# Second matmul layer as seven Strassen products in 32-column tiles of the array

## Chip, cores, metric

One core of one Trainium2 chip. The metric is device time in microseconds (us) of one execution. Ratios between kernels are computed as the mean time of one kernel's fast runs over the mean of the other's of the same rounds, so they are not quite the ratio of the medians quoted here.

## The reference, cut to what matters

```python
# attention part: a causal 7-tap convolution over time, weights by head; gives x (32768 x 192)
def _moe_ref(x, w_in, w_out):          # w_in 192 x 2048, w_out 2048 x 192
    h = x @ w_in
    relu6 = np.clip(h + 3.0, 0.0, 6.0)
    g = h * relu6 / 6.0
    return (g @ w_out).astype(np.float32)
```

Everything is computed in fp32. `w_in` and `w_out` arrive as fp64 and are converted on the chip, in the start.

## The kernel before

The tokens go through in 32 blocks of 1024, each as two halves of 512 (k = 0, 1). A block has two stages. The first layer makes h for 16 chunks of 128 hidden channels; two 64-row tiles of the array run beside each other (431 ns for two records of 593 ns each), one for each half. ScalarE and VectorE turn h into g. The second layer takes 128 tokens of g as the stationary operand (the one that is loaded first, 128 x 128, in 191 ns) and streams 192 columns of `w_out` past it. In this stage VectorE computes the seven taps of the next block's convolution. Matmuls write their sums into PSUM; a bank of it is, in this document, the 512 fp32 columns of one of the program's buffers. ScalarE or VectorE reads them out.

```python
def bank():
    return ps.tile([P, N], F32, name="bank")        # ps: 8 buffers of one PSUM bank each

def h_unit(i, c):                                    # first layer, one chunk
    hs = [bank() for _ in range(G)]
    for s in range(K3):
        for k in range(G):
            r = slice(k * D2, (k + 1) * D2)
            nc.tensor.matmul(out=hs[k][:], lhsT=w_in[r, slots[k], s, :], rhs=y[r, s, :],
                             start=(s == 0), stop=(s == K3 - 1))                        # L223
    for k in range(G):
        r6 = rs.tile([P, N], F32, name="r6")
        nc.scalar.activation(r6[:], hs[k][:], ACT.Relu, bias=half[:], scale=1.0 / 6.0)  # L229
        nc.vector.scalar_tensor_tensor(out=g_tiles[i][k][:, c, :], in0=r6[:], scalar=1.0,
                                       in1=hs[k][:], op0=ALU.min, op1=ALU.mult)         # L232

def unit(t):                                         # second layer, 128 tokens
    o = bank()
    for c in range(NC):
        nc.tensor.matmul(out=o[:, 0:D], lhsT=g[k][:, c, tk * P : (tk + 1) * P],
                         rhs=w_out[:, c, :], start=(c == 0), stop=(c == NC - 1))        # L250
    nc.scalar.copy(out=st["sb"][:, t % TO, :], in_=o[:, 0:D])
    # ... one store of 384 KB after every fourth unit
```

## Time and profile before

| | before |
|---|---|
| median of the first three runs | 2757.02 us (2756.26 to 2757.45) |
| TensorE busy | 2685.9 of 2756.4 us |
| one block in mid-run | 41.40 us first layer + 41.80 us second layer |
| VectorE busy in a block | 33.2 us |
| the rest of the span (start, first block's delay, tail) | 94 us |

TensorE never waits after the start (its 66.6 us of idle time all lie in the first 140 us), so only less TensorE work, or faster streaming, can make the kernel faster. The prediction below shows the lines. In a line of groups one reads: source line, engine, operation, output<-input, shapes, count | busy us, mean ns of one | idle time before and what ended it. PE is TensorE, PEld its weight loads, DVE VectorE, ACT ScalarE, POOL GpSimd.

### The profile page before, as it was taken

The numbers are of one execution on the slowest core, as the hardware profiler recorded it, in microseconds if no ns is written. First come the engines' busy times: TensorE is split into PE (matmuls) and PEld (weight loads), VectorE is DVE, ScalarE is ACT, GpSimd is POOL, SyncE is SP. The second block draws the span as 40 slices with busy tenths as digits, with TensorE's granted clock in tenths as the row PEclk, the third lists the DMA queues.
The fourth block names the chain that finished last, engine by engine and source line by source line (L and its number), as shares of the span: only waits on it lengthen the run. The fifth ranks groups of instructions, "written<-read, shape, count | busy, mean of one in ns | idle before, by whom it ended". The sixth has DMA issues, their size and how long they took to land.

```text
span 2756.4 us, 32856 instructions
## 1 busy us (share of the span) xinstructions
PE 2685.9 (97%) x14336; PEld 1934.2 (70%) x14336; DVE 1096.8 (40%) x1327; ACT 741.2 (27%) x1298; POOL 65.4 (2%) x52
## 2 busy tenths in 40 slices
PE   5599999999999999999999999999999999999999
PEld 2377776677766677766677766677766777766777
DVE  5533344333344233444233444333443333443331
ACT  2222233322233322233322233222233222233222
POOL 3500000000000000000000000000000000000000
PEclk9699999999999999999999999999999999999999
DMA  3200000000000000000000000000000000000000
GB/s 81 69 24 24 17 13 18 24 24 24 11 19 18 24 24 24 7 24 18 24 24 24 7 24 18 23 24 24 7 18 24 24 24 24 7 18 24 12 12 12
DMA packets 54176, 60.57 MB, mean 22 GB/s; under 512 B 2832, under 2 KB 41744, under 8 KB 54032
## 3 DMA queue, kind: packets, MB, share of 16 engines
q1 hardware_dynamic: 48384, 52.17, 6.8%
q10 hardware_dynamic: 5648, 6.30, 0.8%
q8 instruction: 112, 1.84, 0.3%
q14 instruction: 32, 0.26, 0.0%
HBM read 31.72 MB, written 25.17 MB: 21 GB/s over the span
## 4 chain that ended last, share of the span: by engine, by line
PE 96%; POOL 2%; DVE 1%; DMA 1%; issue 0%; ACT 0%; ACTq 0%; POOLq 0%; DVEq 0%
PE bank L250 48%; PE bank L223 48%; POOL scale L132 1%; POOL scale L136 1%; DVE y L199 0%; DMA w_in<-w_in 0%; POOL w_out L151 0%; DVE scale L147 0%; DMA stage<-in_moe_w_in_dram 0%; POOL w_in L151 0%; ACT r L229 0%; DVE g L232 0%; ACTq L76 0%; DVE y L195 0%; DVE scale L128 0%
## 5 line engine op out<-in xcount | busy, mean ns | idle before, releaser
L250 PE MATMUL bank<-w_out,g 128*128 128x192 f32 x8192 | 1349.3, 328 | 29.3 <-POOL w_out L151 29.3
L223 PE MATMUL bank<-y,w_in 64*128 64x512 f32 x6144 | 1340.9, 593 | 37.3 <-DVE y L199 26.1
L250 PEld LDWEIGHTS bank<-w_out,g 128*128 128x128 f32 x8192 | 1336.3, 191 | 57.2 <-POOL w_out L151 33.7
L232 DVE SCALAR_TENSOR_TENSOR g<-r,bank 128x512 f32<-128x512 f32 x1024 | 658.0, 683 | 1563.9 <-ACT r L229 1563.7
L223 PEld LDWEIGHTS bank<-y,w_in 64*128 64x128 f32 x6144 | 597.9, 188 | 760.8 <-issue 743.8
L229 ACT ACTIVATE r<-bank,half 128x512 f32<-128x512 f32 x1024 | 649.7, 684 | 739.7 <-PE bank L223 734.7
L254 ACT COPY o_sb<-bank 128x192 f32<-128x192 f32 x256 | 81.7, 319 | 1237.1 <-PE bank L250 1237.1
L199 DVE SCALAR_TENSOR_TENSOR y<-x,c_sb,y 128x1536 f32<-128x1536 f32 x192 | 349.2, 1819 | 6.8
L195 DVE TENSOR_SCALAR y<-x,c_sb 128x1536 f32<-128x1536 f32 x32 | 57.7, 1802 | 0.0
L132 POOL TENSOR_SCALAR scale<-scale 128x384 uint32<-128x384 uint32 x16 | 25.1, 1569 | 55.6 <-DVE scale L128 55.6
L136 POOL TENSOR_SCALAR scale<-scale 128x384 uint32<-128x384 uint32 x16 | 24.1, 1503 | 1.3
L147 DVE SCALAR_TENSOR_TENSOR scale<-stage,scale 128x384 uint32<-128x384 uint32 x16 | 8.9, 558 | 35.1 <-POOL scale L136 35.1
L127 ACT ACTIVATE rest<-stage 128x384 f32<-128x384 uint32 x16 | 8.7, 549 | 28.5 <-DVE scale L128 17.3
L140 DVE TENSOR_SCALAR top<-stage 128x384 uint32<-128x384 uint32 x16 | 11.3, 703 | 0.0
L144 DVE SCALAR_TENSOR_TENSOR sig<-top,rest 128x384 f32<-128x384 uint32 x16 | 10.6, 660 | 1.6
L151 POOL TENSOR_TENSOR w_out<-sig,scale 128x384 f32<-128x384 f32 x8 | 8.3, 1035 | 5.4 <-DVE scale L147 5.4
L151 POOL TENSOR_TENSOR w_in<-sig,scale 128x384 f32<-128x384 f32 x8 | 8.0, 996 | 5.4 <-DVE scale L147 5.4
L128 DVE TENSOR_SCALAR scale<-stage 128x384 uint32<-128x384 uint32 x16 | 5.6, 353 | 1.2 <-DMA stage<-in_moe_w_in_dram 1.2
L173 ACT ACT_TABLE_LOAD x1 | 1.3, 1283 | 5.5 <-issue 5.5
L168 DVE TENSOR_REDUCE mx<-w_sb 128x1 f32<-128x7 f32 x1 | 0.2, 159 | 6.5 <-DMA w_sb<-in_weight_dram 6.5
L68 DVE MEMSET x<- 64x18 f32 x8 | 0.6, 73 | 0.8 <-PEq L304 0.8
L173 ACT ACTIVATE e_sb<-e_sb 128x7 f32<-128x7 f32 x1 | 0.2, 208 | 1.0 <-DVE e_sb L170 1.0
(10 smaller groups left out, 1.3 us busy)
## 6 DMA issues: line engine op xcount, KB each, us to landing
out_dram<-o_sb SPq DMA_DIRECT2D x64, 384.0 KB, 2.5
x<-in_x_dram SPq DMA_DIRECT2D x56, 388.5 KB, 5.8
x<-in_x_dram SPq DMA_DIRECT2D x8, 384.0 KB, 4.7
stage<-in_moe_w_in_dram ACTq DMA_DIRECT2D x16, 192.0 KB, 3.6
stage<-in_moe_w_out_dram ACTq DMA_DIRECT2D x8, 384.0 KB, 3.1
w_in<-w_in SPq DMA_DIRECT2D x16, 96.0 KB, 2.2
w_sb<-in_weight_dram ACTq DMA_DIRECT2D x2, 1.8 KB
```

Of the source, the lines that this page charges most:

```text
L132: nc.gpsimd.tensor_scalar(out=scale[:], in0=scale[:], scalar1=float((1023 - 127) << 20), scalar2=0.0, op0=ALU.subtract, op1=ALU.max,)
L136: nc.gpsimd.tensor_scalar(out=scale[:], in0=scale[:], scalar1=float(255 << 20), scalar2=8.0, op0=ALU.min, op1=ALU.mult,)
L140: nc.vector.tensor_scalar(out=top[:], in0=high, scalar1=0xFFFFF, scalar2=0x100000, op0=ALU.bitwise_and, op1=ALU.bitwise_or,)
L144: nc.vector.scalar_tensor_tensor(out=sig[:], in0=top[:], scalar=2.0**-20, in1=rest[:], op0=ALU.mult, op1=ALU.add)
L151: nc.gpsimd.tensor_tensor(out=dst, in0=sig[:], in1=scale[:].bitcast(F32), op=ALU.mult)
L195: nc.vector.tensor_scalar(out=y[:], in0=x[:, :, 0:N], scalar1=c, scalar2=None, op0=ALU.mult)
L199: nc.vector.scalar_tensor_tensor(out=y[:], in0=x[:, :, k : k + N], scalar=c, in1=y[:], op0=ALU.mult, op1=ALU.add,)
L223: nc.tensor.matmul(out=hs[k][:], lhsT=w_in[r, slots[k], s, :], rhs=y[r, s, :], start=(s == 0), stop=(s == K3 - 1),)
L229: nc.scalar.activation(r6[:], hs[k][:], ACT.Relu, bias=half[:], scale=1.0 / 6.0)
L232: nc.vector.scalar_tensor_tensor(out=g_tiles[i][k][:, c, :], in0=r6[:], scalar=1.0, in1=hs[k][:], op0=ALU.min, op1=ALU.mult,)
L250: nc.tensor.matmul(out=o[:, 0:D], lhsT=g[k][:, c, tk * P : (tk + 1) * P], rhs=w_out[:, c, :], start=(c == 0), stop=(c == NC - 1),)
L254: nc.scalar.copy(out=st["sb"][:, t % TO, :], in_=o[:, 0:D])
```

## The change

The product g @ w_out is cut two by two: A11, A12 are the two hidden halves of g for the tokens of half 0, A21, A22 those for half 1; B11 to B22 are quarters of `w_out`, C11 to C22 quarters of the result. One level of Strassen's algorithm (in Winograd's form) then needs seven products instead of eight, so 7/8 of the streaming. It pays with four operand sums S1 to S4 on VectorE, four differences T1 to T4 of `w_out` on GpSimd (once), and the sums of the products. Now g moves and `w_out` stands, in pieces of 32 columns, four of them side by side in the array. The result comes out transposed and is turned in 32 x 32 blocks on VectorE. The products come in six groups of matmuls, 0 to 5, each filling one PSUM bank, b[0] to b[5].

```diff
-    ps = ctx.enter_context(tc.tile_pool(name="ps", bufs=8, space=bass.MemoryType.PSUM))
+    ps = ctx.enter_context(tc.tile_pool(name="ps", bufs=4, space=bass.MemoryType.PSUM))
...
+        for o, x, y in ((T1, B12, B11), (T3, B22, B12), (T2, B22, T1), (T4, T2, B21)):
+            nc.gpsimd.tensor_tensor(out=w[:, o], in0=w[:, x], in1=w[:, y], op=ALU.subtract)
...
-    def bank():
-        return ps.tile([P, N], F32, name="bank")
+    def banks():
+        return ps.tile([P, 2, N], F32, name="banks")
...
+    def s_unit(p):                       # after every fourth first-layer unit
+        r = slice(p, p + 2)
+        for o, x, y, op in (
+            (S1, A21, A22, ALU.add), (S3, A11, A21, ALU.subtract),
+            (S2, S1, A11, ALU.subtract), (S4, A12, S2, ALU.subtract),
+        ):
+            nc.vector.tensor_tensor(out=o[:, r], in0=x[:, r], in1=y[:, r], op=op)
+
+    prod = {
+        1: (A11, B11), 2: (A12, B21), 3: (S4, B22), 4: (A22, T4),
+        5: (S1, T1), 6: (S2, T2), 7: (S3, T3),
+    }
...
+                out=bank[j * QS : (j + 1) * QS], lhsT=w_out[:, p, w, cols], rhs=x[:, p],
+                start=(p == ks[0]), stop=(p == ks[-1]), tile_position=(0, j * QS),
...
+        ba, bb, bc = banks(), banks(), banks()
+        b = [t[:, k] for t in (ba, bb, bc) for k in range(2)]
+        def three(k, n, n4, q4):         # three pieces of product n, one of product n4
+            side_by_side(*[out_mm(b[k], q, n, q, every) for q in range(NQ)],
+                         out_mm(b[k], NQ, n4, q4, every))
...
+        three(0, 1, 2, 0)
+        nc.scalar.copy(out=p1[:], in_=b[0][m])
+        piece(p2, 0, b[0], NQ)           # ScalarE copy of 32 rows
+        three(1, 5, 2, 1)
+        piece(p2, 1, b[1], NQ)
+        for u in conv:
+            u()
+        three(2, 7, 2, 2)
+        piece(p2, 2, b[2], NQ)
+        ...                              # sum, transpose and store of C11
+        three(3, 6, 4, 0)
+        ...                              # copy, four sums that read b[3], b[2], b[1]; store of C22
+        three(4, 3, 4, 1)
+        piece(p4, 1, b[4], NQ)
+        add(u2[:], u2[:], b[4][m])
+        ...                              # store of C12; last piece of product 4 into b[5], C21
```

The first layer's unit writes both halves into one two-bank buffer, with one ReLU and one product 1024 wide; g, x and y are kept in one buffer each.

More of the change, by code (lines that the diff above doesn't have):

```diff
@@ L50 @@
     assert H * GJ == D2 and K3 * GJ == GS and G == 2 and S % TB == 0 and DFF % P == 0 and PAD <= N
-    cst = ctx.enter_context(tc.tile_pool(name="cst", bufs=1))
-    xs = ctx.enter_context(tc.tile_pool(name="xs", bufs=2))
-    ys = ctx.enter_context(tc.tile_pool(name="ys", bufs=2))
-    gs = ctx.enter_context(tc.tile_pool(name="gs", bufs=G + 1))
-    rs = ctx.enter_context(tc.tile_pool(name="rs", bufs=3))
-    os_ = ctx.enter_context(tc.tile_pool(name="os", bufs=2))
-    stg = ctx.enter_context(tc.tile_pool(name="stg", bufs=3))
-    cnv = ctx.enter_context(tc.tile_pool(name="cnv", bufs=2))
-    ps = ctx.enter_context(tc.tile_pool(name="ps", bufs=8, space=bass.MemoryType.PSUM))
+    NP = NC // 2
+    DH = D // 2
+    QS = 32
+    NQ = DH // QS
+    assert NQ * QS == DH and NQ == 3 and P // QS == 4
+    cst = ctx.enter_context(tc.tile_pool(name="cst", bufs=1))
+    xs = ctx.enter_context(tc.tile_pool(name="xs", bufs=1))
+    ys = ctx.enter_context(tc.tile_pool(name="ys", bufs=1))
+    rs = ctx.enter_context(tc.tile_pool(name="rs", bufs=2))
+    ps = ctx.enter_context(tc.tile_pool(name="ps", bufs=4, space=bass.MemoryType.PSUM))
+    start_pools = ExitStack()
+    stg = start_pools.enter_context(tc.tile_pool(name="stg", bufs=3))
+    cnv = start_pools.enter_context(tc.tile_pool(name="cnv", bufs=2))
     def load_x(i):
@@ L86 @@
     w_in = cst.tile([P, NC, K3, P], F32, name="w_in")
-    w_out = cst.tile([P, NC, D], F32, name="w_out")
+    w_out = cst.tile([P, NP, 8, DH], F32, name="w_out")
+    B11, B12, B21, B22, T1, T2, T3, T4 = range(8)
     w_in_bits = moe_w_in.bitcast(U32).rearrange("(p s) (c f w) -> c p s f w", s=K3, f=P, w=2)
-    w_out_bits = moe_w_out.bitcast(U32).rearrange("(c p) w -> p c w", p=P)
-    WO = 2
+    w_out_bits = moe_w_out.bitcast(U32).rearrange("(k c p) w -> p c k w", p=P, k=2)
     WS = K3 * P
-    assert WO * D == WS
+    assert 2 * D == WS
     def stage():
@@ L102, in load_w_in @@
                 out=st[half * D2 : (half + 1) * D2].rearrange("p (s f) w -> p s (f w)", s=K3),
-                in_=w_in_bits[2 * j + half].rearrange("p s f w -> p s (f w)"),
+                in_=w_in_bits[j + half * NP].rearrange("p s f w -> p s (f w)"),
             )
@@ L109, in load_w_out @@
         nc.scalar.dma_start(
-            out=st[:].rearrange("p (c d) w -> p c (d w)", c=WO),
-            in_=w_out_bits[:, j * WO : (j + 1) * WO],
+            out=st[:].rearrange("p (k d) w -> p k (d w)", k=2), in_=w_out_bits[:, j]
         )
@@ L153, in w_in_unit @@
     def w_in_unit(j):
-        own, other = j, NC // 2 + j
+        own, other = j, NP + j
         to_f32(w_in[:, own].rearrange("p s f -> p (s f)"), w_in_st.pop(j))
@@ L159, in w_out_unit @@
     def w_out_unit(j):
-        dst = w_out[:, j * WO : (j + 1) * WO, :].rearrange("p c d -> p (c d)")
-        to_f32(dst, w_out_st.pop(j))
+        w = w_out[:, j]
+        to_f32(w[:, B11 : B22 + 1].rearrange("p b d -> p (b d)"), w_out_st.pop(j))
+        for o, x, y in ((T1, B12, B11), (T3, B22, B12), (T2, B22, T1), (T4, T2, B21)):
+            nc.gpsimd.tensor_tensor(out=w[:, o], in0=w[:, x], in1=w[:, y], op=ALU.subtract)
     w_in_st, w_out_st = {}, {}
@@ L204, in conv_units @@
         return [lambda k=k: tap(k) for k in range(KC)]
-    g_tiles = {}
-    def bank():
-        return ps.tile([P, N], F32, name="bank")
+    g = cst.tile([P, NP, 2, G, N], F32, name="g")
+    A11, A21, A12, A22 = (g[:, :, h, k] for h in range(2) for k in range(G))
+    s_t = cst.tile([P, 3, NP, N], F32, name="s")
+    S1, S2, S4 = (s_t[:, j] for j in range(3))
+    S3 = A21
+    def banks():
+        return ps.tile([P, 2, N], F32, name="banks")
     def h_unit(i, c):
         y = y_tiles[i]
-        slots = [c // 2 + (c % 2 != k) * (NC // 2) for k in range(G)]
-        hs = [bank() for _ in range(G)]
+        slots = [c % NP + (c // NP != k) * NP for k in range(G)]
+        h = banks()
         for s in range(K3):
@@ L223, in h_unit @@
                 nc.tensor.matmul(
-                    out=hs[k][:], lhsT=w_in[r, slots[k], s, :], rhs=y[r, s, :],
+                    out=h[:, k], lhsT=w_in[r, slots[k], s, :], rhs=y[r, s, :],
                     start=(s == 0), stop=(s == K3 - 1),
                 )
-        for k in range(G):
-            r6 = rs.tile([P, N], F32, name="r6")
-            nc.scalar.activation(
-                r6[:], hs[k][:], ACT.Relu, bias=half[:], scale=1.0 / 6.0
-            )
-            nc.vector.scalar_tensor_tensor(
-                out=g_tiles[i][k][:, c, :], in0=r6[:], scalar=1.0, in1=hs[k][:],
-                op0=ALU.min, op1=ALU.mult,
-            )
@@ L237, in out_units @@
-    def out_units(i):
-        g = g_tiles.pop(i)
-        rows = out[i * TB : (i + 1) * TB, :].rearrange("(t p) d -> p t d", p=P)
-        TO = NT // 2
-        st = {}
-        def unit(t):
-            if t % TO == 0:
-                st["sb"] = os_.tile([P, TO, D], F32, name="o_sb")
-            o = bank()
-            k, tk = divmod(t, N // P)
-            for c in range(NC):
-                nc.tensor.matmul(
-                    out=o[:, 0:D], lhsT=g[k][:, c, tk * P : (tk + 1) * P],
-                    rhs=w_out[:, c, :], start=(c == 0), stop=(c == NC - 1),
-                )
-            nc.scalar.copy(out=st["sb"][:, t % TO, :], in_=o[:, 0:D])
-            if t % TO == TO - 1:
-                nc.sync.dma_start(out=rows[:, t + 1 - TO : t + 1, :], in_=st["sb"][:])
-        return [lambda t=t: unit(t) for t in range(NT)]
+        r6 = rs.tile([P, G, N], F32, name="r6")
@@ new lines, in h_unit @@
+        nc.scalar.activation(r6[:], h[:], ACT.Relu, bias=half[:], scale=1.0 / 6.0)
+        nc.vector.scalar_tensor_tensor(
+            out=g[:, c % NP, c // NP], in0=r6[:], scalar=1.0, in1=h[:],
+            op0=ALU.min, op1=ALU.mult,
+        )
+    def s_unit(p):
[5 more added lines that the diff above has]
+            nc.vector.tensor_tensor(out=o[:, r], in0=x[:, r], in1=y[:, r], op=op)
@@ new lines, with out_mm @@
+    prod = {
+        1: (A11, B11), 2: (A12, B21), 3: (S4, B22), 4: (A22, T4),
+        5: (S1, T1), 6: (S2, T2), 7: (S3, T3),
+    }
+    def out_mm(bank, j, n, q, ks):
+        x, w = prod[n]
+        cols = slice(q * QS, (q + 1) * QS)
+        return [
+            lambda p=p: nc.tensor.matmul(
+                out=bank[j * QS : (j + 1) * QS], lhsT=w_out[:, p, w, cols], rhs=x[:, p],
+                start=(p == ks[0]), stop=(p == ks[-1]), tile_position=(0, j * QS),
+            )
+            for p in ks
+        ]
@@ new lines, in side_by_side, with out_phase, piece, add @@
+    def side_by_side(*streams):
+        for mms in zip(*streams):
+            for mm in mms:
+                mm()
+    def out_phase(i, conv):
+        every = range(NP)
+        ba, bb, bc = banks(), banks(), banks()
+        b = [t[:, k] for t in (ba, bb, bc) for k in range(2)]
+        def three(k, n, n4, q4):
+            side_by_side(
+                *[out_mm(b[k], q, n, q, every) for q in range(NQ)],
+                out_mm(b[k], NQ, n4, q4, every),
+            )
+        def piece(dst, q, src, j):
+            nc.scalar.copy(
+                out=dst[q * QS : (q + 1) * QS], in_=src[j * QS : (j + 1) * QS]
+            )
+        def add(out, x, y, op=ALU.add):
+            nc.vector.tensor_tensor(out=out, in0=x, in1=y, op=op)
+        def store(c, k, half_):
+            xt = ot.tile([DH, N], F32, name="xt")
+            nc.vector.transpose(out=xt[:], in_=c)
+            t0 = i * TB + k * N
+            rows = out[t0 : t0 + N, half_ * DH : (half_ + 1) * DH].rearrange(
+                "(t r) (q d) -> q r t d", r=QS, d=QS
+            )
+            for q in range(NQ):
+                nc.sync.dma_start(
+                    out=rows[q],
+                    in_=xt[q * QS : (q + 1) * QS].rearrange("r (t d) -> r t d", d=QS),
+                )
+        m = slice(0, DH)
+        p1, p2, p4, u2, u3, c22 = (cs.tile([DH, N], F32, name=f"c{k}") for k in range(6))
+        three(0, 1, 2, 0)
[7 more added lines that the diff above has]
+        piece(p2, 2, b[2], NQ)
+        add(p2[:], p1[:], p2[:])
+        store(p2[:], 0, 0)
+        three(3, 6, 4, 0)
+        piece(p4, 0, b[3], NQ)
+        add(u2[:], p1[:], b[3][m])
+        add(u3[:], u2[:], b[2][m])
+        add(u2[:], u2[:], b[1][m])
+        add(c22[:], u3[:], b[1][m])
+        store(c22[:], 1, 1)
+        three(4, 3, 4, 1)
+        piece(p4, 1, b[4], NQ)
+        add(u2[:], u2[:], b[4][m])
+        store(u2[:], 0, 1)
+        n = NP // 4
+        side_by_side(*[out_mm(b[5], j, 4, 2, range(j * n, (j + 1) * n)) for j in range(4)])
+        piece(p4, 2, b[5], 0)
+        last = p4[2 * QS : 3 * QS]
+        for j in range(1, 4):
+            add(last, last, b[5][j * QS : (j + 1) * QS])
+        add(u3[:], u3[:], p4[:], ALU.subtract)
+        store(u3[:], 1, 0)
@@ L265 @@
         for i in range(NB):
-            g_tiles[i] = [gs.tile([P, NC, N], F32, name="g") for _ in range(G)]
-            conv = conv_units(i + 1) if i + 1 < NB else []
-            for c in range(NC):
-                if i == 0 and c % 2 == 0:
-                    j = c // 2
-                    if j + 2 < NC // 2:
-                        w_in_st[j + 2] = load_w_in(j + 2)
-                    else:
-                        w_out_st[j + 2 - NC // 2] = load_w_out(j + 2 - NC // 2)
-                    if j + 1 < NC // 2:
-                        w_in_unit(j + 1)
-                h_unit(i, c)
-            y_tiles.pop(i)
+            for p in range(NP):
+                if i == 0:
+                    if p + 2 < NP:
+                        w_in_st[p + 2] = load_w_in(p + 2)
+                    else:
+                        w_out_st[p + 2 - NP] = load_w_out(p + 2 - NP)
+                    if p + 1 < NP:
+                        w_in_unit(p + 1)
+                h_unit(i, p)
+                h_unit(i, NP + p)
+                if p % 2:
+                    s_unit(p - 1)
+            y_tiles.pop(i)
+            if i == 0:
+                for j in range(NP):
+                    if j + 2 < NP:
+                        w_out_st[j + 2] = load_w_out(j + 2)
+                    w_out_unit(j)
+                start_pools.close()
+                cs = ctx.enter_context(tc.tile_pool(name="cs", bufs=1))
+                ot = ctx.enter_context(tc.tile_pool(name="ot", bufs=4))
+            out_phase(i, conv_units(i + 1) if i + 1 < NB else [])
             if i + 2 < NB:
                 x_tiles[i + 2] = load_x(i + 2)
-            if i == 0:
-                for j in range(NC // WO):
-                    if j + 2 < NC // WO:
-                        w_out_st[j + 2] = load_w_out(j + 2)
-                    w_out_unit(j)
-            for t, u in enumerate(out_units(i)):
-                u()
-                for v in conv[t * len(conv) // NT : (t + 1) * len(conv) // NT]:
-                    v()
 _INS = ['x', 'weight', 'moe_w_in', 'moe_w_out']
```

## The prediction

> **What bounds the kernel now.** I read the page's busy times first, then the groups, then the busy times by window for one whole block (1024 tokens), then the waits.
>
> ```profile
> PE 2685.9 (97%) x14336; PEld 1934.2 (70%) x14336; DVE 1096.8 (40%) x1327; ACT 741.2 (27%) x1298; POOL 65.4 (2%) x52
> L250 PE MATMUL bank<-w_out,g 128*128 128x192 f32 x8192 | 1349.3, 328 | 29.3 <-POOL w_out L151 29.3
> L223 PE MATMUL bank<-y,w_in 64*128 64x512 f32 x6144 | 1340.9, 593 | 37.3 <-DVE y L199 26.1
> ```
>
> TensorE is busy for 97% of the span, split evenly between the first layer (L223) and the second (L250), and its only idle time, 29.3 + 37.3 us, is in the start. The windows of one block in mid-run (first layer, then second) give the period:
>
> ```profile
> 256.50:297.90 41.40, 41.40 (x194) 18.51 (x193) 19.27 (x30) 19.30 (x31) 0.00 (x0) 1.00 0.11 29
> 297.90:339.70 41.80, 41.80 (x260) 41.58 (x258) 13.93 (x10) 3.50 (x9) 0.00 (x0) 1.00 0.03 10
> ```
>
> The columns are length, then the busy time of PE, weight loads, VectorE, ScalarE and GpSimd, the clock, DMA. A block is 41.40 + 41.80 = 83.20 us with TensorE never idle at full clock; VectorE needs 33.20 of it. 32 blocks are 2662 us; the other 94 us of the 2756.4 us span are the start (weight conversion[...]) and the tail.
>
> **Rates.** There are two records per source matmul: the second layer has 32 x 8 x 16 = 4096 source matmuls and 8192 records. A first-layer record streams 512 columns for 64 rows, and two row tiles run abreast: 192 records in 41.40 us is 431 ns per pair. A second-layer record streams 192 columns over the full array in 41.80/256 = 163 ns. Per streamed column that is 0.84 and 0.85 ns: both run at the same rate.
>
> [...] The trace agrees on independence for the two row tiles (431 ns for two records whose mean is 593 ns), and the mode change between the layers, already there twice a block, shows no idle time in the two windows. [...] loads for the full array are busy 41.58 of 41.80 us beside an unbroken PE. [...] After a DMA wait in the first block, a window 0.2 us wide has two records starting:
>
> ```profile
> 43.81 1.22 PE L223 MATMUL bank<-y,w_in 64*128 64x512 f32 x2 [2.25 <-DMA w_in<-w_in]
> ```
>
> In program order the second of them is the other half of the same matmul, on the same tile, and has to follow the first, as the two records at 40.44 did (1.12 us together). Here they run beside each other, so one belongs to the other tile and has passed it. No run here has column tiles. [...] The new stores have 128 B runs.
>
> **The change, part by part.** *TensorE, second layer.* One level of Strassen needs 7 of 8 products. Each has 8 chunks and three 32-column pieces: 7 x 24 = 168 source matmuls a block. Four side by side make 42 slots (5 groups of 8, and 2 for the last piece split by chunks), each of two records of 512 columns. If four column tiles run abreast as two row tiles do, a slot is 2 x 431 = 862 ns and the layer 42 x 0.862 = 36.2 us for 41.8: 5.6 us less a block, 179 us in all. The first layer's TensorE work does not change.
>
> *VectorE, first layer.* [...] Two PSUM banks per unit and four buffers let TensorE run ahead: VectorE's 5 us of sums cover two units. So it just fits, and nothing of it should sit on the path.
>
> *VectorE, second layer.* The last sums end 7 us or so after the first layer, beside the first product group (6.9 us). The taps (12.7 us from the present rows, 7 x 1.82) end at 20 us. Six [96 x 512] sums and three transposes of about 0.7 us come in time. After the last matmul one copy, three 32-row adds, a subtraction and a transpose remain, some 4 us, beside the next block's first unit, whose first product could start only after 2.6 + 1.2 us anyway. VectorE per block: 20 + 20 + 13 + 7 + 3 = 63 us of 78.
>
> *Stores.* Twelve of 64 KB for two of 384 KB; 196,608 packets of 128 B. The present queue moves 48,384 packets in 6.8% of its engines' time, so even four times that, about 27%, is off the path. x is loaded after its only buffer was read, 40 us before it is needed.
>
> *Start.* The eight weight units each get four 96-wide subtractions on GpSimd. From 1.035 us for 384, about 0.33 us each: 8 x 1.3 = 10 us on the chain that now stalls L250. The sums join VectorE's in-order queue in the first block, eight batches' share 8 x 2.5 = 20 us, of which I take half as exposed: 10 us. *Tail.* 4 us.
>
> **Sum.** 32 x (41.4 + 36.2) = 2483; plus the old start and tail 94, plus 20 and 4: 2601. I add 0.4 us a block for small waits between products and sums, where VectorE is nearly full: 2614 us, 5% faster.
>
> **The rivals.**
>
> *A: column tiles do not run four abreast.* Each source matmul is two records in sequence on one tile. If starts are strictly in order over column tiles, the second record of tile 0 waits for the first and holds tiles 1 to 3 back. Then only two are abreast: 42 x 4 x 0.431 = 72.4 us a layer, 30.6 us more a block, 3700 us or so. For it: [...] column tiles share all their rows, so four streams must be read from the same partitions at once, which nothing in the trace does. Against it: row tiles do pass each other[...]. That is the large doubt: 20%.
>
> *B: the instruction rate binds.* Now there are 256 records and as many loads in 41.8 us (82 ns each), and in the new layer 336 + 336 in 36.2 us: 54 ns each. The trace shows no such rate held. [...] Against it: two loads and two matmuls start within 0.1 us in the first block, though they may have been queued. 10%.
>
> *C: weight loads do not hide.* A load of 128 columns takes 188 to 191 ns and 256 of them fit 41.8 us. There are eight in a 862 ns slot; if one of 32 columns cost as much and they were serial, 1.5 us a slot, far slower. They are a quarter as wide and four tiles should load beside each other. Counted with A and B.
>
> *D: VectorE becomes the bound of the first layer.* At 1.4 us a sum, the four units need 10.5 us: 0.2 us each lost, 20 to 30 us in all. That only shaves the gain: 2640.
>
> **Range and chances.** If the tiles run abreast (about two in three), the result lies between 2580 (no small waits, a start only 5 us longer) and 2660 (D and a start 30 us longer). B or part of C gives 2700 to 2800. A gives well above 3000. So the prediction is 2614; 2580 to 2790 should hold 8 times in 10; faster by 2% (under 2702) 0.67, within 2% 0.11, slower 0.22.
>
> **What would show it.** Right: second-layer windows of some 36.5 us with 336 records, PE without gaps, PE as the chain's only long line, first-layer windows still at 41.4 to 41.8 with VectorE over 90% busy. Wrong by A: windows of 70 us, a slot of four tiles taking 1.7 us instead of 0.86. By B: 336 records in 41 us, starts evenly spread at about 120 ns. By C: weight loads as busy as PE with gaps in it. By D: PE waiting on the VectorE product in the first layer.

An estimate from the profile before: a tap of 1536 columns takes 1.82 us, in proportion 1.21 us for 1024, and two 512-wide products one after the other took 1.28 us (at 1042.35 us), two such ReLUs 1.27 us. At 1.21 to 1.28 us each, four products and four sums are 9.7 to 10.2 us, 94 to 99% of the 10.35 us of four units; four sums are 4.8 to 5.1 us, and the first block's sixteen 19 to 20 us, the 8 x 2.5 of the start. (The 0.33 us of a difference is an estimate too: 0.10 us, which GpSimd's one-column memsets take, and a quarter of the rest of the 1.035 us.)

The sum came to 2614 us. Rival B's figure gave about 2790 us, the top of the range. An estimate: if the 672 records of the new layer take the 41.80 us of the old one, the sum is 2614 + 32 x 5.6 = 2793 us. As to the start: in the profile before, the granted clock was 0.83 from 25 to 99 us and 0.52 from 99 to 140 us.

## The result

| | before | after |
|---|---|---|
| median, 4 runs each | 2756.64 us | 2744.34 us |
| profiled span | 2756.4 us | 2742.7 us |
| first layer, mid-run | 41.40 us | 41.40 us |
| second layer, mid-run | 41.80 us | 40.24 us |
| block | 83.20 us | 81.64 us |
| first block's first layer | 73.3 us | 93.6 us |
| first block's second layer | 73.9 us | 83.5 us |
| tail: from the last second layer's first matmul to the end, less the mid-run length of that layer | 3.9 us | 8.2 us |

The ratio is 0.9957 (95% interval 0.994 to 0.9975): a real gain, of 0.4%. The layers' lengths are the distances between their first matmuls in the trace. The table closes: 31 blocks of 1.56 us less are 48.4 us, the first block costs 29.9 more, the tail 4.3, and TensorE starts 0.3 later; 13.9 us less, and the spans differ by 13.7.

The page after has, for the three lines shown of before, these:

```profile
PE 2530.7 (92%) x16896; PEld 933.7 (34%) x16896; DVE 1969.1 (72%) x1775; ACT 710.2 (26%) x754; POOL 81.6 (3%) x84
L240 PE MATMUL banks<-y,w_in 64*128 64x512 f32 x6144 | 1345.2, 594 | 47.9 <-DVE y L211 26.4
L271 PE MATMUL banks<-g,w_out 128*32 128x512 f32 x6144 | 1188.6, 598 | 91.4 <-POOL w_out L161 46.0
L271 PE MATMUL banks<-s,w_out 128*32 128x512 f32 x4608 | 673.4, 594 | 64.6 <-ACT c L295 64.6
```

TensorE's busy time fell by 155 us, not far from the 179 that the eighth promised (the two L271 groups overlap and must not be added). But TensorE is now idle for 212 us of the span instead of 70. The windows of one block (first layer, then second; columns as in the prediction) put that idle time in the second layer:

```profile
1020.00:1061.40 41.40, 41.40 (x198) 18.51 (x195) 35.01 (x33) 17.28 (x16) 0.00 (x0) 1.00 0.15 29
1061.40:1101.70 40.30, 36.86 (x340) 10.56 (x338) 25.49 (x22) 4.60 (x7) 0.00 (x0) 1.00 0.07 12
```

36.86 us of work in 40.30. And the narrow timeline shows four tiles starting together, each four records some 0.43 us after the four before (two such sets are a slot of the prediction; columns: start, length, instruction group, idle before):

```profile
1002.77 0.63 PE L271 MATMUL banks<-s,w_out 128*32 128x512 f32 x3 [0.70 <-ACT c L295]
1002.79 0.62 PE L271 MATMUL banks<-g,w_out 128*32 128x512 f32 x1
1003.23 0.60 PE L271 MATMUL banks<-s,w_out 128*32 128x512 f32 x3
1003.25 0.59 PE L271 MATMUL banks<-g,w_out 128*32 128x512 f32 x1
```

So the doubtful part of the plan, four column tiles abreast, holds. What fails is seen in the chain of waits of the same block (start, length, what the end of the run hung on):

```profile
1061.46 7.08 PE banks L271 x64
...
1068.56 0.58 ACT c L319
...
1069.15 0.59 ACT c L295
...
1069.78 13.98 PE banks L271 x128
...
1083.79 0.59 ACT c L295
...
1084.42 13.98 PE banks L271 x128
...
1098.43 0.59 ACT c L295
...
1099.04 0.70 DVE c L300
...
1099.78 1.92 PE banks L271 x16
```

TensorE stops three times in a block, for 1.3, 0.7 and 1.4 us. Group 1 starts when ScalarE has copied group 0 out of PSUM; group 3 starts when group 2's fourth tile has been copied; the last group starts when group 4 has been copied and added. Groups 2 and 4 do not stop. The six groups have two banks to a buffer: the groups that stop are exactly those that write the *second* bank of a buffer whose first bank was written just before. The data do not ask for it: group 1 reads nothing that the copies write, and it writes another bank than they read. Over the run TensorE's waits of this kind are:

```profile
PE banks L271 <- ACT c L295: 64.6, 64, 1.4
PE banks L271 <- POOL w_out L161: 46.0, 8, 12.6
PE banks L271 <- DVE c L300: 45.4, 32, 1.4
```

The first and the third row are 110 us, 3.4 us a block; the second is the start, and was 29.3 before.

### The profile page after: what moved, and what is told of

Same layout as the page of the kernel before. It is cut to its first block, busy times and chain, and to the rows that moved or that the text cites. A ratio compares the mean times of both kernels' runs of the same rounds, so it can differ in the third digit from the quotient of the medians.

```text
span 2742.7 us, 37945 instructions
## 1 busy us (share of the span) xinstructions
PE 2530.7 (92%) x16896; PEld 933.7 (34%) x16896; DVE 1969.1 (72%) x1775; ACT 710.2 (26%) x754; POOL 81.6 (3%) x84
## 3 DMA queue, kind: packets, MB, share of 16 engines
q1 hardware_dynamic: 217344, 52.19, 10.3%
## 4 chain that ended last, share of the span: by engine, by line
PE 91%; ACT 3%; DVE 3%; POOL 2%; issue 1%; DMA 0%; ACTq 0%; DVEq 0%
PE banks L240 48%; PE banks L271 43%; ACT c L295 2%; DVE c L300 1%; POOL scale L146 1%; POOL scale L142 1%; ACT c L319 1%; POOL w_out L173 0%; DVE y L211 0%; DVE s L258 0%; POOL w_out L161 0%; DVE scale L157 0%; DVE g L246 0%; DMA stage<-in_moe_w_in_dram 0%; DVE g L258 0%
## 5 line engine op out<-in xcount | busy, mean ns | idle before, releaser
L240 PE MATMUL banks<-y,w_in 64*128 64x512 f32 x6144 | 1345.2, 594 | 47.9 <-DVE y L211 26.4
L271 PE MATMUL banks<-g,w_out 128*32 128x512 f32 x6144 | 1188.6, 598 | 91.4 <-POOL w_out L161 46.0
L240 PEld LDWEIGHTS banks<-y,w_in 64*128 64x128 f32 x6144 | 597.8, 188 | 794.8 <-issue 750.3
L245 ACT ACTIVATE r<-banks,half 128x1024 f32<-128x1024 f32 x512 | 570.5, 1114 | 822.2 <-PE banks L240 613.6
L246 DVE SCALAR_TENSOR_TENSOR g<-r,banks 128x1024 f32<-128x1024 f32 x512 | 615.7, 1218 | 201.4 <-ACT r L245 190.1
L271 PE MATMUL banks<-s,w_out 128*32 128x512 f32 x4608 | 673.4, 594 | 64.6 <-ACT c L295 64.6
L271 PEld LDWEIGHTS banks<-g,w_out 128*32 128x32 f32 x6144 | 306.6, 110 | 459.2 <-issue 302.3
L300 DVE TENSOR_TENSOR c<-c,banks 96x512 f32<-96x512 f32 (+1 forms) x256 | 172.5, 684 | 377.5 <-ACT c L295 373.1
L271 PEld LDWEIGHTS banks<-s,w_out 128*32 128x32 f32 x4608 | 183.5, 110 | 546.0 <-issue 413.5
L258 DVE TENSOR_TENSOR g<-g 128x1024 f32<-128x1024 f32 x128 | 156.9, 1226 | 4.4
```

The costliest lines, as they stand in the source:

```text
L240: nc.tensor.matmul(out=h[:, k], lhsT=w_in[r, slots[k], s, :], rhs=y[r, s, :], start=(s == 0), stop=(s == K3 - 1),)
L245: nc.scalar.activation(r6[:], h[:], ACT.Relu, bias=half[:], scale=1.0 / 6.0)
L246: nc.vector.scalar_tensor_tensor(out=g[:, c % NP, c // NP], in0=r6[:], scalar=1.0, in1=h[:], op0=ALU.min, op1=ALU.mult,)
L258: nc.vector.tensor_tensor(out=o[:, r], in0=x[:, r], in1=y[:, r], op=op)
L271: lambda p=p: nc.tensor.matmul(out=bank[j * QS : (j + 1) * QS], lhsT=w_out[:, p, w, cols], rhs=x[:, p], start=(p == ks[0]), stop=(p == ks[ ...
L300: nc.vector.tensor_tensor(out=out, in0=x, in1=y, op=op)
```

## The experiments

My theory: waits are set by the buffer, not by the bank, so sharing a two-bank PSUM buffer between consecutive groups costs the stops; and two additions to the start (operand sums on VectorE, differences on GpSimd) cost another 15 us more than I had put down. The rival for the first: a new group has to wait until the group before it has been copied out of PSUM (its evacuation), whatever buffer it has. The runs are compared with 2744.34 us after and some 2757 us before (in each set of runs the kernel before gave a median of 2757.2).

### Banks dealt out over four buffers

```diff
-        ba, bb, bc = banks(), banks(), banks()
-        b = [t[:, k] for t in (ba, bb, bc) for k in range(2)]
+        ta, tb, tc_, td = banks(), banks(), banks(), banks()
+        b = [ta[:, 0], td[:, 0], tb[:, 0], ta[:, 1], tc_[:, 0], td[:, 1]]
```

> The changed kernel with its six product banks dealt out over four two-bank buffers, so that the bank that a product group writes shares a buffer only with a bank whose readers have long finished. Nothing else changes: same instructions, same sums. Theory (the second bank of a two-bank PSUM buffer waits until the copies and sums that read the first bank are done): the waits of TensorE on the copies and sums, 64.6 + 45.4 us in the changed kernel, go to under 10 us, the second-layer window goes from 40.3 to 36.9 us, and the time from 2744 to about 2635 us. Rival (the groups wait because a new accumulation group needs the evacuation to be over, or an engine is late, whatever buffer it is): the gaps of 1.3, 0.7 and 1.4 us stay and the time stays within 1% of 2744 us.

Measured: 2614.52 us, ratio to before 0.9484 (0.947 to 0.9498). The windows (second layer, then first) and the chain of that block:

```profile
1016.50:1052.70 36.20, 36.20 (x340) 10.83 (x338) 25.06 (x22) 4.60 (x7) 0.00 (x0) 1.00 0.07 12
1052.70:1094.10 41.40, 41.40 (x200) 18.51 (x196) 35.43 (x33) 17.29 (x16) 0.00 (x0) 1.00 0.15 29
```

```profile
1016.56 36.19 PE banks L271 x336
1052.75 41.39 PE banks L240 x191
```

TensorE does not stop at all, and no wait of TensorE on the copies or sums is left in the list of waits. The rival falls: with the buffers apart the six groups follow one another without idle time, 36.20 us busy in 36.20. The gain, 129.8 us, is more than the 110 us of waiting. A block is 4.05 us shorter, of which 3.44 was waiting; the other 0.6 us, 0.2 for each stop, is counted as busy (36.86 against 36.20): the 64 records of group 0 take 7.08 us before a stop, and 64 of these unbroken 336 in 36.19 us are 6.89. I call it run-out; that it is the end of the last matmuls is my estimate, from a record's 592 ns against the 431 ns between two on a tile.

### One of the three pairs kept

```diff
-        ba, bb, bc = banks(), banks(), banks()
-        b = [t[:, k] for t in (ba, bb, bc) for k in range(2)]
+        ta, tb, tc_, td = banks(), banks(), banks(), banks()
+        b = [ta[:, 0], ta[:, 1], td[:, 0], tb[:, 0], tc_[:, 0], td[:, 1]]
```

> A dose: of the three places where a product group shares a buffer with the group before it only the first is kept (groups 0 and 1 in one two-bank buffer), the others apart. Expected by the theory: one gap of 1.3 us a block, [...] 32 x 1.5 = 49 us over the banks-only kernel's 2614.5: about 2664 us, second-layer window 37.7 us. By the rival (a gap anywhere drains into others) either 2614 or 2744.

(The 1.5 us is an estimate from the run before: the gap of 1.3 and the 0.2 us of run-out.)

Measured: 2664.10 us (2 runs), ratio 0.9662. The chain has the first stop and no other:

```profile
1033.90 7.07 PE banks L271 x64
...
1041.00 0.58 ACT c L319
...
1041.59 0.59 ACT c L295
...
1042.23 29.39 PE banks L271 x272
```

The block's second layer takes 37.72 us, 1.53 more than with none. This kernel too has four buffers, so it was the pairing, and not the fourth buffer, that mattered. The wait stands in the program: in the trace of the changed kernel the first weight load of group 1 waits for a semaphore, a counter between engines, that the copy of 1069.15 us raises, and it starts at 1069.78 us, 0.05 us after the copy's end; in the banks-only run TensorE's waits name no copy and no sum. What in the building of the program draws it was not looked into. That it goes by buffer is shown for these two-bank PSUM buffers alone. For buffer s, which is in SBUF, it did not hold: in the banks-only run group 1 starts to read S1 out of s at 1023.38 us while VectorE is writing S4 into another part of s, until 1023.90 us, as two lines of its timeline show:

```profile
1022.67 1.23 DVE L258 TENSOR_TENSOR s<-g,s 128x1024 f32<-128x1024 f32 x1
1023.38 0.60 PE L271 MATMUL banks<-s,w_out 128*32 128x512 f32 x3
```

### Operand sums of the first block later

```diff
-                if p % 2:
+                if p % 2 and i > 0:
                     s_unit(p - 1)
...
                     w_out_unit(j)
+                    if j % 2:
+                        s_unit(j - 1)
```

> The changed kernel with the operand sums of the first block taken out of its first layer and put beside the conversion of w_out; a correct result. Theory (VectorE works in order, so the sums stand in front of the weight conversion on which the first layer waits): the first layer of the first block, which runs from 25 to 120 us, ends some 20 us earlier, near the 99 us of the kernel before, and the time falls from 2744 to about 2725 us. Rival (the longer start comes from the wider ReLU and product [...]): no change of the time, or the sums only move and lengthen the w_out stage by as much.

Measured: 2736.02 us, ratio 0.9924. Half of the theory and half of the rival are right. The windows of the first block's two layers, after and then in this run:

```profile
26.40:120.00 93.60, 59.59 (x192) 24.11 (x192) 53.23 (x66) 22.04 (x24) 32.39 (x24) 0.79 0.22 57
120.00:203.50 83.50, 46.51 (x336) 10.12 (x336) 34.88 (x43) 6.67 (x12) 45.00 (x53) 0.68 0.12 29
```

```profile
26.20:97.00 70.80, 53.60 (x192) 22.69 (x192) 34.12 (x50) 22.03 (x24) 32.37 (x24) 0.88 0.29 76
97.00:192.40 95.40, 47.07 (x336) 10.23 (x336) 56.58 (x59) 6.67 (x12) 56.20 (x53) 0.66 0.10 26
```

The first layer is 22.8 us shorter: the sums had stood wholly on its path. But the next stage is 11.9 us longer, because there they stand in front of the next unit's first VectorE step: the last steps of the eight conversions start 6.7 and 10.2 us apart in turn, where in the changed kernel all were 6.7 us apart.

### Differences of w_out later

```diff
-        for o, x, y in ((T1, B12, B11), (T3, B22, B12), (T2, B22, T1), (T4, T2, B21)):
-            nc.gpsimd.tensor_tensor(out=w[:, o], in0=w[:, x], in1=w[:, y], op=ALU.subtract)
+    def diff_units():                    # called once, after the eight conversions
+        for o, x, y in ((T1, B12, B11), (T3, B22, B12), (T2, B22, T1), (T4, T2, B21)):
+            for j in range(NP):
+                w = w_out[:, j]
+                nc.gpsimd.tensor_tensor(out=w[:, o], in0=w[:, x], in1=w[:, y], op=ALU.subtract)
```

> The changed kernel with the 32 differences of w_out on GpSimd after all eight conversions instead of four after each; a correct result. Theory (they lengthen each step of the conversion chain, 6.7 us instead of 4.9): the stage in which the first products wait for w_out is 12 to 15 us shorter, and the time about 2731 us. Rival (they fill idle time of GpSimd, and the chain is slower for VectorE's sake): under 4 us.

Measured: 2733.98 us, ratio 0.9916. TensorE's wait for `w_out` falls from 46.0 to 33.2 us, and the first block's second layer from 83.5 to 72.1 us. In the same run its first layer, which the edit does not touch, came out 2.1 us longer, so the profiled spans differ by 9.2 us and not by 11.4; the medians differ by 10.4. The conversions' last steps start 4.88 us apart, as before the change.

### All three

> The three edits together: banks apart, sums later, differences later. If the three costs are separate places on TensorE's path, the gains add: 109 + 20 + 13 us off 2744, so about 2602 us, 5.6% faster than the kernel before. If removing the gaps uncovers VectorE as the bound (60 of a block's 78 us busy), the first-layer window grows past 41.4 us and the time stays over 2630 us.

Its edit is the three diffs above together. Measured: 2599.75 us, ratio 0.9429 (0.9415 to 0.9443). The expected 2602 is met, but not by the same terms: the banks gave 130 and not 109, and the two edits to the start together gave 14.8 on top, less than the 18.7 of their separate gains. VectorE does not become the bound: the first layer stays at 41.40 us. But the first block's second layer takes 85.3 us here against 78.5 in the banks-only run.

### Sums of the first block inside the conversion's own wait

```diff
-    def to_f32(dst, st):
+    def to_f32(dst, st, between=None):
...
+        if between:                      # VectorE would wait here for GpSimd's scale
+            between()
         nc.vector.scalar_tensor_tensor(
             out=scale[:], in0=high, scalar=0x80000000, in1=scale[:],
...
-        to_f32(w[:, B11 : B22 + 1].rearrange("p b d -> p (b d)"), w_out_st.pop(j))
+        to_f32(w[:, B11 : B22 + 1].rearrange("p b d -> p (b d)"), w_out_st.pop(j),
+               lambda: s_unit(j - j % 2, slice(0, 2) if j % 2 == 0 else slice(2, 4)))
```

> The three edits together, with the first block's sums two at a time between the VectorE steps of one w_out unit where it waits some 3 us for GpSimd, instead of four after every second unit; a correct result. Theory (in the run with all three edits the sums still stand in front of the next unit's first step, so the w_out stage is 85 us long instead of the 78 of the banks-only kernel): the stage gets about 10 us shorter and the time falls from 2600 to about 2590 us. Rival (GpSimd's own work, 4 us a unit, sets the pace): within 3 us of 2600.

Measured: 2585.28 us, ratio 0.9376 (0.9362 to 0.939), the fastest kernel, with a correct result. The stage takes 71.0 us, 14 less than with all three edits, and the first block's two layers 143.8 us together, against 147.2 in the kernel before. The sums are not quite free: the conversions' last steps start 5.20 us apart, against 4.88 without sums.

```profile
26.70:99.40 72.70, 56.74 (x194) 23.03 (x194) 36.62 (x52) 22.02 (x24) 32.73 (x25) 0.84 0.29 74
99.40:170.40 71.00, 46.58 (x336) 10.41 (x336) 52.74 (x57) 6.68 (x12) 51.21 (x53) 0.71 0.13 34
```

### The tiles without Strassen

The product table, sums and differences are taken out. The core of the edit:

```diff
-        x, w = prod[n]
+    # output half hf of tokens k, all 16 chunks: eight plain products
-                out=bank[j * QS : (j + 1) * QS], lhsT=w_out[:, p, w, cols], rhs=x[:, p],
+                out=bank[j * QS : (j + 1) * QS], lhsT=w_out[:, p, 2 * h + hf, cols],
+                rhs=g[:, p, h, k],
...
+        b = [banks()[:, 0] for _ in range(NQ)]      # one bank of each buffer
```

> The changed kernel without Strassen: the plain eight products, 192 source matmuls a block in four 32-column tiles, transposed on VectorE and stored as in the change, one bank per buffer so that no group waits for another's readers; no operand sums and no differences. It tells what the tiles, the transposed form and the 128 B stores do by themselves. Expected: 48 slots of 862 ns, 41.4 us a block for the second layer against 41.8 before and 36.2 with seven products; VectorE some 37 us a block; time 2740 to 2765 us, the same as before. If the tiles or the stores had a cost of their own that Strassen's eighth pays for, it would be over 2780 us.

Measured: 2742.68 us, ratio 0.995 (0.9933 to 0.9966). The window of the second layer:

```profile
1037.36:1078.70 41.34, 41.34 (x387) 12.38 (x385) 15.18 (x10) 3.44 (x5) 0.00 (x0) 1.00 0.06 11
```

48 slots take 41.34 us and 42 take 36.19: the eighth is worth 5.15 us a block, 165 us in all. The tiles, the transposed result and the short stores neither gain nor lose much: 0.46 us a block against 41.80. This kernel and the changed one take the same time within 2 us. So in the kernel as changed, all that Strassen saved went into the three stops a block and the longer start: of 160 us in 31 blocks the stops took 126, and the first block is 35 us longer than here (177.1 against 142.4 us).

## Why the prediction was wrong

The time, 2744 us, lies inside the stated range, but the forecast was 5% faster and the result is 0.4% faster, and none of the rivals leads there. That the range held is luck: it reached to 2790 us for rivals B and C, and neither happened.

**The step that failed** is "I add 0.4 us a block for small waits between products and sums". In its place there were 3.44 us of waiting and 0.6 us of run-out: 4.05 us a block. I had looked at who would be late (VectorE), and asked whether each sum would come "in time" for the data. I did not ask what the first matmul of each group would wait for on the side of its output buffer. The diff had it: the kernel before gave every accumulation its own one-bank buffer, and the change makes two-bank buffers and fills them with consecutive groups. The banks-only and the one-pair runs show the wait and its dose.

**TensorE's work.** Right to the last digit that counts: 42 slots were to take 36.2 us and take 36.19 where nothing stops them. The first layer stays at 41.40.

**Rival A**, in-order starts: wrong, given 20%. Four tiles start together and 336 records take 36.19 us, 431 ns for four, as two row tiles had taken 431 ns for two. **Rival B**, instruction rate: wrong. 672 records of matmuls and loads in 36.19 us are 54 ns each, and hold. **Rival C**, loads: wrong; they are busy for 10.83 of 36.20 us beside an unbroken TensorE (110 ns each for 32 columns, against 190 for 128). **Rival D**, VectorE in the first layer: wrong as a bound. The sums took 1.22 us and the wide product 1.22 us, the lower end of the estimate beside the prediction; in the first layer VectorE is busy 35.0 to 35.4 of 41.4 us, 85%, and not over 90%, because the last four sums of a block, 4.9 us, and its last product run in the next stage, which I had myself placed there.

**Start.** Mis-sized. I took 20 us for the sums, half of them exposed, and 10 us for the differences. The first layer of the first block grew by 20.3 us, and moving the sums out gave back 22.8: they were wholly exposed (sixteen sums take 19.6 us; in the shorter stage the granted clock was also higher, 0.88 against 0.79). Moving the differences gave 11.4 us off its stage. I had counted that VectorE had idle time there, which it has; but it works in order, and the idle time lay behind the steps that the chain waited for. (With all three edits, the next conversion's first step starts at 123.2 us, as the last of the four sums begun at 117.8 ends.) The run with the sums inside the conversion's wait puts them into that idle time, and then they cost some 0.3 us a conversion, 2.6 us in all.

**Tail and stores.** The tail was to be 4 us longer and is 4.3. The stores are off the path: those of 64 KB in runs of 128 B landed in 2.0 us (384 KB before: 2.5 us), and the queue has 10.3% of its engines' time, far less than the 27% that I had set as a ceiling.

**The sum.** Measured against 2614: 31 blocks with 3.64 us more than the 78.0 expected are 113 us, the first block 15 us more than expected. That the banks-only kernel lands on 2614.5 is partly luck: the 0.4 us a block that it does not have and the longer start are about as large.

## What to carry to other kernels

When work is regrouped, list for each new group not only what it reads but which buffer it writes, who still reads any part of that buffer, and when they finish; here a PSUM buffer of two banks filled by consecutive groups made the second wait for the first's readers, 3.44 us a block in three such places. Work added to an engine with idle time is nearly free only if it is placed, in that engine's order, where the engine would have waited: here the first block's sums, 19.6 us of VectorE, cost 2.6 us there, and 22.8 us of the first layer where they first stood. And a small gain of a large change should be split into what was saved and what was given back before the change is dropped: here two lines of buffer assignment were worth 130 us.
